# A state-space scan in front of routed experts: the operands B and C turned by TensorE, the two halves of the product matrix interleaved

## The chip, the cores and the metric

One core of one Trainium2 chip runs the kernel. The metric is device time in microseconds (us) of one execution. The kernel is one launch; nothing is computed on the host.

## What is computed

The first half is a state-space scan (Mamba-2 style) over 4 batches x 8 heads x 768 tokens with head size D = 32 and state size N = 16; the second half sends each of the 3072 tokens to one of 8 experts, by a hash of its id.

```python
log_a = np.log(np.clip(a, 1e-06, 1.0))
for c in range(nc):                                   # chunks of tokens
    cum = np.cumsum(la, axis=-1)
    L = np.exp(cum[..., :, None] - cum[..., None, :]) * causal
    M = einsum('bhin,bhjn->bhij', Cc, Bc) * L
    y = M @ xc + einsum('bhin,bhnd->bhid', Cc, state) * exp(cum)
    state = exp(sum(la)) * state + sum_j B_j x_j exp(cum[-1] - cum_j)
x = y.transpose(0, 2, 1, 3).reshape(3072, 256)
expert_idx = token_ids * 2654435761 % 8
out[mask_e] = np.maximum(x[mask_e] @ w1[e], 0) @ w2[e]   # w1 256x1024, w2 1024x256
```

## The kernel before, in words

**Scan.** The kernel works in units of T = 64 tokens. Two units make a product step k (128 tokens, `NPR` = 6 of them), two product steps make a load step ck (CT = 256 tokens, `CK` = 3). A unit's decay factors exp(-cum) and exp(cum) are multiplied into the rows of B and C (`scale_rows`, L206, line of the operation L208), so that the decay mask falls out of the product.

The decays: `a` is loaded as 96 rows (batch, head, ck) of 256 tokens (L104). DVE clips it, ACT takes the log, DVE makes running sums (L188) and centres them (L191), 32 small TensorE products bring them to the layout of B and C (L196) and ACT makes `fac` (L201, L202). Two ACT table loads stand in this chain.

B and C (`raw`, L110 to L113) lie with tokens on the partitions. They are scaled, then turned by DVE's 32x32 stream transposes into `bt` and `ct` (`turn_rows`, L218); ACT makes from `ct` two copies `ce` in which the even or the odd head of a pair is zeroed (`mask_c`, L224). After this turn, the 32 partitions of strip b hold batch b, and 4 column groups g hold pairs of heads. B is also needed with tokens as rows: eight DMAs per load step, issued on ACT's queue, copy the scaled rows to `ben` (`shuffle_b`, L229).

A product step then has these parts on TensorE, all fp32, each matmul call being two records in the trace:
- `gram` (L503): 32 calls, 32 rows x 64 columns of the array, 128 moving columns: C times B. The order is g, u (unit), b, so that eight tiles of the array (four strips b, two column halves u) are used in turn.
- `masked` (L508): one DVE instruction copies the causal part of four PSUM banks to `m_sb`.
- `dstates` (L521): 32 calls, new state contributions; ACT evicts `d_sb` (L527); `states` on DVE (L537, L540) chains the states z.
- `intra` (L556): 64 calls of 64x64, 32 moving columns; m times x.
- `inter` (L568): 64 calls of 32x64, 32 moving columns, one a head: masked C times z.
- `y_evict` on ACT (L575), `y_store` on SP's DMA queue (L578) to `y_dram`.

The order is written out by hand (L580 to L669): in step k, `states(k)`, `masked(k+1)`, `intra(k)`, `inter(k)`, `y_evict(k)`, a piece of the routing, after k = 0 and k = 2 the turn of the next load step, `gram(k+2)`, `dstates(k+1)`. Each engine executes its instructions in this order. POOL scales the rows of load steps 1 and 2. x is loaded as four DMAs per 128 tokens on SP (L118).

**Routing.** Between the steps, DVE, POOL and TensorE count the tokens of each expert, sort the experts by size, give each token a slot, and build the tables `idx_in` and `idx_out` (L259 to L420): ids, counts (before k = 0), prefix (k = 0), places and ranks (k = 1), slots, lanes and tiles (k = 2), the table product (L396) and the index arithmetic (k = 3). Seven gathers of early tiles (`EK`, tokens of the first 2048 rows of y) are issued on POOL after step 4 in program order (L664); after the scan TensorE turns them (`turn_pair`, L467).

**Experts.** From L745 on, the experts' two layers are done by a Strassen scheme with seven products per 2x2 block (`up` L745, `down` L790; sums on DVE and POOL, L701 to L726), weights loaded on SP (L435, L439). The weight loads after the first few wait for the gather of the late tiles, by a small DMA `held` (L866). Its end is a scatter of the output rows on POOL (L826). This part is in the change only at its start.

Each TensorE result lands in one of eight PSUM banks of 128 x 512 fp32: `gram` in 0 to 3, y in 4 to 7, `dstates` in halves of 6 and 7.

Of the kernel before, what the change touches and what calls it, by code (L numbers as in the profile page):

```python
# [9 lines left out]
F32 = mybir.dt.float32  # L10
# [15 lines left out]
def kernel(  # L26
# [61 lines left out]
    BM, BY, BD, SP = 0, 4, 6, 256  # L88
# [15 lines left out]
    tok = apre.tile([NCH, P, 2], I32)  # L106
    raw, xs = {}, {}

    def load_rows(ck, i, eng):
        t = raw[ck, i] = aload.tile([P, H, RR * NS], F32, name=f"raw{i}")  # L110
        for b in range(NB):
            src = (B, C)[i][b, :, ck * CT:(ck + 1) * CT, :].rearrange("h (p r) n -> p h (r n)", r=RR)
            eng.dma_start(out=t[32 * b:32 * b + 32], in_=src)  # L113

    def load_x(k):
        t = xs[k] = xload.tile([P, NB, H, D], F32, name="x_t")
        for b in range(NB):
            sp_e.dma_start(out=t[:, b], in_=x[b, :, k * P:(k + 1) * P, :].rearrange("h t d -> t h d"))  # L118

    load_rows(0, 0, sp_e)  # L120
    load_rows(0, 1, act)
    act.dma_start(out=tok, in_=tok_h.bitcast(I32).rearrange("(c p two) -> c p two", c=NCH, two=2))
    load_x(0)
    load_x(1)

    fill16 = const.tile([P, 512], BF16)
    dve.memset(fill16, 0.0)
    rst = apre.tile([P, CT // T, T], F32)
# [4 lines left out]
    m_sb = [awork.tile([P, NB, G * 2 * T], F32, name=f"m{i}", bufs=1) for i in range(2)]  # L133
    ident = const.tile([P, P], F32)
    make_identity(nc, ident)
    dve.memset(m_sb[0], 0.0)
    cmask = apre.tile([P, 2 * G, T], F32)
    pool_e.memset(cmask, 1.0)
    for u in range(2):
        pool_e.affine_select(out=cmask[u * T:(u + 1) * T], in_=cmask[u * T:(u + 1) * T], pattern=[[0, 2 * G], [1, T]],  # L140
                             compare_op=OP.is_ge, fill=0.0, base=0, channel_multiplier=-1)
    par = apre.tile([P, 2], F32)
    dve.tensor_reduce(out=par, in_=ident.rearrange("q (b e n) -> q e b n", b=NB, e=2), axis=AX.XY, op=OP.add)
    rep = apre.tile([NA, NB * 2, NS], F32)
    reph = apre.tile([NA, NB * 2], F32)
    idn = ident[0:NA, 0:NA].rearrange("q (b g e c) -> q b g e c", b=NB, g=G, e=2)
    for b in range(NB):
        dve.tensor_reduce(out=reph[:, 2 * b:2 * b + 2], in_=idn[:, b].rearrange("q g e c -> q e g c"), axis=AX.XY,
                          op=OP.add)
# [887 lines left out]
```

## Time and profile before

| what | us |
|---|---|
| median of 3 runs | 297.62 (297.23 to 301.02) |
| profiled execution, its time | 296.71 |
| its span, first to last instruction | 295.0 |
| around the span | 1.71 |
| PE busy | 232.9 (79%) |
| DVE / POOL / ACT busy | 194.0 / 166.7 / 72.2 |

An engine is busy while one of its instructions executes; idle time before an instruction is put down to what released it. PEld is TensorE's weight load, which runs beside PE. PEclk, or the granted clock, is a share of 2.4 GHz; it has two levels, 1.0 and 0.5 (1.2 GHz), and values between are means.

### The profile page before, as it was taken

To read this page: it belongs to the slowest core of one execution; us is meant where nothing else is said; L and a number is where in the kernel's file an instruction comes from. 1 tells how busy PE (TensorE), PEld (TensorE's weight loads), DVE (VectorE), ACT (ScalarE), POOL (GpSimd) and SP (SyncE) were. 2 spreads that over 40 slices of the span, in tenths; PEclk is the share of its full clock that TensorE was granted. 3 is DMA by queue.
4 is the path that set the end of the run, shared out by engine and by line. 5 is a ranking of instruction groups with operands and counts; after the bars stand their busy time and mean duration, and the time that the engine had idled before them with its cause. 6 is when DMAs were issued, how large, how long until landed. Compare 5 with 4: busy or idle time off the path is not lost.

```text
span 295.0 us, 7905 instructions
## 1 busy us (share of the span) xinstructions
PE 232.9 (79%) x3314; PEld 217.4 (74%) x3315; DVE 194.0 (66%) x316; ACT 72.2 (24%) x152; POOL 166.7 (57%) x181
## 2 busy tenths in 40 slices
PE   6347579270695588969799989999999998699980
PEld 2136469270594477959799989999999898699870
DVE  4758829369156110427987997896878979876710
ACT  2330221010311012644122123223242340342110
POOL 5304204138604500649995997999969999064123
PEclk9655555555559555999999999999999999999998
DMA  8999983734005322498418164292141421220001
GB/s 166 153 175 143 174 175 79 145 110 144 2 6 174 97 76 74 124 292 317 158 31 289 39 195 164 54 298 76 37 155 42 115 105 37 84 78 36 20 35 56
DMA packets 53371, 34.87 MB, mean 118 GB/s; under 512 B 27068, under 2 KB 47668, under 8 KB 53334
## 3 DMA queue, kind: packets, MB, share of 16 engines
q1 hardware_dynamic: 46242, 25.69, 33.5%
q0 software_dynamic: 2400, 6.43, 6.7%
q10 hardware_dynamic: 4692, 2.22, 4.3%
q8 instruction: 27, 0.44, 0.6%
q14 instruction: 10, 0.08, 0.1%
HBM read 26.47 MB, written 6.42 MB: 111 GB/s over the span
## 4 chain that ended last, share of the span: by engine, by line
PE 40%; DVE 21%; DMA 17%; issue 9%; ACT 4%; POOL 3%; SPq 2%; ACTq 2%; POOLq 0%; DVEq 0%
PE ps L745 13%; PE ps L790 13%; DMA out_dram<-o_sb,idx_out 9%; DVE t L710 4%; PE ps L568 4%; DMA w<-in_moe_w_dram 4%; DVE m L508 3%; PE ps L556 3%; PE ps L503 3%; ACT ce L224 2%; DMA raw<-in_C_dram 2%; DMA x_t<-in_x_dram 2%; ACTq L229 2%; PE ps L521 2%; SPq L118 1%
## 5 line engine op out<-in xcount | busy, mean ns | idle before, releaser
L447 POOL DMA_INDIRECT xg<-y_tokens,idx_in x25 | 29.2, 1169 | 36.7 <-DMA y_tokens<-y_sb 18.0
L701 POOL TENSOR_TENSOR s<-w 128x512 f32<-128x512 f32 x30 | 38.7, 1292 | 13.3 <-DMA w<-in_moe_w_dram 12.9
L826 POOL DMA_INDIRECT out_dram<-o_sb,idx_out x25 | 29.1, 1164 | 25.4 <-ACT o_sb L822 17.7
L745 PE MATMUL ps<-t,s 128*128 128x202 f32 (+7 forms) x192 | 37.2, 327 | 1.6 <-DVE u L760 1.6
L790 PE MATMUL ps<-t,s 128*128 128x202 f32 (+7 forms) x192 | 35.3, 326 | 0.2 <-DVE t L722 0.2
L745 PEld LDWEIGHTS ps<-t,s 128*128 128x128 f32 x192 | 31.6, 189 | 2.2 <-issue 1.9
L790 PEld LDWEIGHTS ps<-t,s 128*128 128x128 f32 x192 | 31.8, 189 | 0.4 <-issue 0.4
L556 PE MATMUL ps<-x_t,m 64*64 64x32 f32 x768 | 22.4, 282 | 9.4 <-ACT d_sb L527 5.7
L556 PEld LDWEIGHTS ps<-x_t,m 64*64 64x64 f32 x768 | 20.7, 209 | 11.4 <-ACT d_sb L527 6.2
L503 PE MATMUL ps<-ce,bt 32*64 32x128 f32 x384 | 13.2, 416 | 20.0 <-ACT ce L224 18.5
L503 PEld LDWEIGHTS ps<-ce,bt 32*64 32x64 f32 x384 | 10.8, 209 | 21.0 <-ACT ce L224 19.2
L745 PE MATMUL ps<-xT,w 128*128 128x202 f32 (+7 forms) x128 | 24.5, 327 | 1.6 <-DMA w<-in_moe_w_dram 1.6
L568 PE MATMUL ps<-z,ce 32*64 32x32 f32 x704 | 20.5, 290 | 3.0 <-issue 3.0
L537 DVE TENSOR_TENSOR zd<-d_sb,z 128x256 f32<-128x256 f32 x10 | 4.2, 425 | 27.5 <-ACT d_sb L527 27.4
L745 PEld LDWEIGHTS ps<-xT,w 128*128 128x128 f32 x128 | 21.0, 190 | 1.8 <-issue 1.8
L568 PEld LDWEIGHTS ps<-z,ce 32*64 32x64 f32 x704 | 18.7, 217 | 4.4 <-issue 4.0
L710 DVE TENSOR_TENSOR t<-xT 128x202 f32<-128x202 f32 (+7 forms) x16 | 19.2, 1198 | 4.0 <-ACT xT L461 4.0
L701 POOL TENSOR_TENSOR s<-w,s 128x512 f32<-128x512 f32 x15 | 20.4, 1363 | 0.2
L701 POOL TENSOR_TENSOR s<-s,w 128x512 f32<-128x512 f32 x15 | 19.9, 1325 | 0.7
L575 ACT ACTIVATE y_sb<-ps 128x1024 f32<-128x1024 f32 x6 | 6.1, 1024 | 50.4 <-PE ps L568 50.4
L208 POOL TENSOR_TENSOR rows<-raw,fac 128x1024 f32<-128x1024 f32 x5 | 10.7, 2149 | 13.3 <-DMA raw<-in_C_dram 8.8
L773 ACT ACTIVATE hx<-hx 128x404 f32<-128x404 f32 (+7 forms) x16 | 8.2, 524 | 40.6 <-DVE hx L772 36.8
(178 smaller groups left out, 460.2 us busy)
## 6 DMA issues: line engine op xcount, KB each, us to landing
w<-in_moe_w_dram SPq DMA_DIRECT2D x16, 512.0 KB, 8.0
w<-in_moe_w_dram SPq DMA_DIRECT2D x8, 1024.0 KB
x_t<-in_x_dram SPq DMA_DIRECT2D x24, 128.0 KB, 4.6
y_tokens<-y_sb SPq DMA_DIRECT2D x6, 512.0 KB, 2.9
raw<-in_B_dram SPq DMA_DIRECT2D x12, 128.0 KB, 3.3
ben<-rows ACTq DMA_DIRECT2D x24, 64.0 KB, 2.4
raw<-in_C_dram SPq DMA_DIRECT2D x8, 128.0 KB, 4.0
raw<-in_C_dram ACTq DMA_DIRECT2D x4, 128.0 KB
```

Of the source, the lines that this page charges most:

```text
L208: eng.tensor_tensor(out=t.rearrange("q r (h n) -> q r h n", h=H), in0=raw[ck, i].rearrange("q h (r n) -> q r h n", r=RR), in1=fac[:, i].re ...
L447: pool_e.indirect_dma_start(out=xg[k], out_offset=None, in_=y_dram[0:n, :], in_offset=bass.IndirectOffsetOnAxis(ap=idx_in[:, k:k + 1], axi ...
L503: pe.matmul(out=ps[u * T:(u + 1) * T, BM + b, g * P:(g + 1) * P].rearrange("q (e i) -> q e i", e=2), lhsT=bts[ck][r, g, c], rhs=ces[ck][r, ...
L508: dve.copy_predicated(out=m_sb[k % 2], mask=cmask.bitcast(I32).rearrange("q j i -> q (j i)").unsqueeze(1).to_broadcast([P, NB, 2 * G * T]) ...
L556: pe.matmul(out=o, lhsT=m_sb[k % 2][u * T:(u + 1) * T, b, h * T:(h + 1) * T], rhs=xs[k][u * T:(u + 1) * T, b, h], start=first, stop=True, ...
L568: pe.matmul(out=o, lhsT=ces[ck][r, h // 2, h % 2, kk * P + u * T:kk * P + (u + 1) * T], rhs=zs[2 * k + u][r, h * D:(h + 1) * D], start=fir ...
L701: eng.tensor_tensor(out=s[:, i], in0=a_, in1=b_, op=o)
L710: dve.tensor_tensor(out=t[:, i], in0=a_, in1=b_, op=OP.subtract)
L745: pe.matmul(out=ps[:, bank, i * n:(i + 1) * n], lhsT=lhs[:, (q0 + i) * P:(q0 + i + 1) * P], rhs=rhs, start=(first and i == 0), stop=True, ...
L773: act.activation(hq(2), hq(2), AF.Relu)
L790: pe.matmul(out=ps[:, bank, 0:n], lhsT=lhs(q), rhs=rhs(q), start=(first and q == 0), stop=True, skip_group_check=True)
L826: st = pool_e.indirect_dma_start(out=out[:], out_offset=bass.IndirectOffsetOnAxis(ap=idx, axis=0), in_=o_sb, in_offset=None, bounds_check= ...
```

## The change

B and C are turned by full 128x128 transposes on TensorE (`squares`), eight for each of B and C in a load step, and evicted from PSUM by ACT or DVE (`take_b`, `take_c`), the masking of the even or odd head being done in the eviction. Batches and pairs of heads change places: the strip of 32 partitions now is the pair g, and the column group is the batch. B with tokens as rows comes from eight more transposes of `bt` (`steps_b`) instead of DMAs. The decays are computed in the layout of B and C (running sums over 8 tokens on each partition, then two products that add what lies before); so `a` is loaded by four DMAs with rows of 8 tokens (32 bytes) instead of one. The even/odd masking for the states is in `gm`, so `inter` needs one call for two heads: 32 calls of 64 moving columns in place of 64 of 32. `gram` and `masked` are cut in two halves, g = 2, 3 and g = 0, 1 (`two_halves`; `between(k)` is `intra(k, (0, 1))`), and in even steps each half of `gram(k+1)` stands between halves of `intra(k)`. POOL makes most constants and zeroes `m_sb`. x is one DMA per 128 tokens. The token ids are loaded first and counted before the decays; the routing is cut in nine pieces (6 is the table product, 7 makes `idx_in`), the seven early gathers stand after step 3, and the last two groups of early turns among the first expert products. `w2` moves to another pool.

```diff
-    a_t = apre.tile([NA, CT], F32)
-    act.dma_start(out=a_t, in_=a.rearrange("b h (c t) -> (b h c) t", c=CK))
+    act.dma_start(out=tok, ...)
+    a_t = apre.tile([P, H, CK, RR], F32)
+    for b in range(NB):
+        (sp_e, act)[b % 2].dma_start(out=a_t[32 * b:32 * b + 32],
+                                     in_=a[b].rearrange("h (c p r) -> p h c r", c=CK, r=RR))
...
+        sp_e.dma_start(out=t.rearrange("q b h d -> q (b h) d"),
+                       in_=x[:, :, k * P:(k + 1) * P, :].rearrange("b h t d -> t (b h) d"))
     load_rows(0, 0, sp_e)
-    load_rows(0, 1, act)
+    load_rows(0, 1, sp_e)
     load_x(0)
+    load_rows(1, 0, sp_e)
+    load_rows(1, 1, sp_e)
     load_x(1)
+    load_x(2)
...
+    def decays_b():
+        dve.tensor_tensor_scan(out=f2(cum), data0=rst..., data1=f2(a_t), initial=0.0, op0=OP.mult, op1=OP.add)
+        dve.tensor_copy(out=cnt..., in_=ps[:, 6, 0:2 * E * NCH])
+        pe.matmul(out=ps[:, 3, 0:NA], lhsT=ident, rhs=f2(cum), start=True, stop=False, skip_group_check=True)
+        pe.matmul(out=ps[:, 3, 0:NA]..., lhsT=wsel[:, 0]...,
+                  rhs=f3(cum)[:, :, RR - 1:RR].to_broadcast([P, HC, RR]), start=False, stop=True, ...)
+        for i in range(2):
+            act.activation(f2(fac[:, i]), ps[:, 3, 0:NA], AF.Exp, scale=(-1.0, 1.0)[i])
...
-        dve.transpose(out=t.rearrange("q g (p r) -> q g r p", r=RR),
-                      in_=rows[ck, i].rearrange("q r (g f) -> q g r f", g=G))
-            act.activation(ces[ck][:, :, e], cts[ck], AF.Copy, scale=par[:, e:e + 1])
-            eng.dma_start(out=t[:, j], in_=rows[ck, 0][16 * j:16 * j + 16])
+    def squares(ck, i, r0=0, r1=RR, bank=None):
+        for r in range(r0, r1):
+            pe.transpose(out=ps[:, bank + r // 4, (r % 4) * P:(r % 4 + 1) * P], in_=rows[ck, i][:, r], identity=ident)
...
+    def gram(k, gs=(0, 1, 2, 3)):
         for b in range(NB):
+            for u in range(2):
+                for g in gs:
+                    r = slice(32 * g, 32 * g + 32)
+                    pe.matmul(out=ps[u * T:(u + 1) * T, GB + g, b * P:(b + 1) * P]..., lhsT=bts[ck][r, b, c],
+                              rhs=ces[ck][r, :, b, c], start=True, stop=True, skip_group_check=True)
...
+    def intra(k, gs=(2, 3, 0, 1)):
+        for g in gs:
+            for b in range(NB):
+                for e in range(2):
+                    for u in range(2):
+                        r = slice(u * T, (u + 1) * T)
+                        pe.matmul(out=ps[r, YB + g, (2 * b + e) * D:(2 * b + e + 1) * D],
+                                  lhsT=m_sb[k % 2][r, g, b, e * T:(e + 1) * T], rhs=xs[k][r, b, 2 * g + e], ...)
+    def inter(k):
+        for u in range(2):
+            for b in range(NB):
+                for g in range(G):
+                    pe.matmul(out=ps[u * T:(u + 1) * T, YB + g, 2 * b * D:2 * (b + 1) * D],
+                              lhsT=cts[ck][r, b, kk * P + u * T:kk * P + (u + 1) * T],
+                              rhs=zs[2 * k + u][r, b]..., ...)
...
+    def two_halves(k, inner=None):
+        gram(k, (2, 3))
+        masked(k, 2, 4)
+        if inner:
+            inner()
+        gram(k, (0, 1))
+        masked(k, 0, 2)
...
     for k in range(NPR):
+        states(k)
+        if k % 2 == 0:
+            intra(k, (2, 3))
+            two_halves(k + 1, lambda: between(k))
+            inter(k)
+            y_evict(k)
+            y_store(k)
+            if k + 2 < NPR:
+                squares(ck + 1, 1)
+                take_c(ck + 1, 0, act)
+                squares(ck + 1, 0)
+                take_b(ck + 1)
+            dstates(k + 1)
...
+        else:
+            intra(k)
+            if nxt:
+                steps_b(ck + 1, GB, 0, 4)
+            inter(k)
+            y_evict(k)
+            y_store(k)
+            if k == 3:
+                piece(6)
+                piece(7)
+            if nxt:
+                two_halves(k + 1)
...
+                dstates(k + 1)
...
+        if k == 3:
             for q in EK:
                 gather(q, early=True)
...
+    load_w1(0, 1)
+    early(0)
+    early(1)
     a_ctx.close()
...
     for m, (what, i) in enumerate(seq):
+        if m == 3:
+            early(2)
+        if m == 6:
+            early(3)
```

## Rows read from the trace of the kernel before

**Rows 1.** Three stretches: us, busy (instructions) per engine, granted clock, DMA share, GB/s.

```profile
0.00:20.70 20.70, 9.15 (x86) 4.40 (x87) 13.40 (x37) 6.07 (x11) 6.94 (x40) 0.72 1.01 162
20.70:115.40 94.70, 61.77 (x2232) 55.82 (x2232) 48.26 (x87) 14.53 (x19) 30.70 (x38) 0.54 0.48 106
115.40:295.00 179.60, 161.93 (x996) 157.19 (x996) 132.32 (x192) 51.59 (x124) 129.05 (x103) 0.98 0.37 119
```

**Rows 2.** The same view, four stretches of the scan (PE, PEld, DVE, ACT, POOL).

```profile
33.40:38.20 4.80, 0.01 (x2) 0.01 (x3) 2.51 (x2) 3.20 (x3) 0.00 (x0) 0.50 0.95 192
51.80:58.00 6.20, 0.86 (x14) 0.58 (x8) 1.63 (x7) 0.59 (x1) 0.70 (x1) 0.50 0.76 120
64.70:76.10 11.40, 0.00 (x0) 0.00 (x0) 8.23 (x16) 3.21 (x3) 9.22 (x17) 0.50 0.32 93
92.30:102.40 10.10, 4.25 (x73) 3.25 (x73) 4.33 (x7) 0.00 (x0) 7.25 (x7) 0.61 0.33 99
```

**Rows 3.** The chain that ended last, pieces in the scan: start, us, what.

```profile
35.95 2.19 ACT ce L224 x2
53.93 3.47 DMA ben<-rows
92.27 2.84 issue
```

**Rows 4.** Timeline of the start: start, us, engine, line, operation.

```profile
4.86 0.23 DVE L184 TENSOR_SCALAR a_t<-a_t 96x256 f32<-96x256 f32 x1
5.79 1.28 ACT L132 ACT_TABLE_LOAD   x1 [5.79 <-DMA raw<-in_C_dram]
10.55 1.23 DVE L208 TENSOR_TENSOR rows<-raw,fac 128x1024 f32<-128x1024 f32 x1 [1.42 <-ACT fac L201]
20.70 2.02 PE L503 MATMUL ps<-ce,bt 32*64 32x128 f32 x64 [2.19 <-ACT ce L224]
```

**Rows 5.** DMA: the queue of SP's loads (packets, MB, share); a stretch of input loads.

```profile
q1 hardware_dynamic: 46242, 25.69, 33.5%
...
21.00:31.00 10.00, 8.52 (x315) 7.50 (x306) 7.98 (x8) 0.72 (x2) 4.26 (x3) 0.50 0.98 154
```

**Rows 6.** Groups by line and shape, 0 to 120 us.

```profile
L568 PE MATMUL ps<-z,ce 32*64 32x32 f32 x704 | 20.5, 290 | 3.0 <-issue 3.0
L503 PE MATMUL ps<-ce,bt 32*64 32x128 f32 x384 | 13.2, 416 | 20.0 <-ACT ce L224 18.5 <-DVE m L508 1.5
```

**Rows 7.** Timeline of PE and PEld: transposes, and products at both levels of the clock.

```profile
38.19 2.01 PE L503 MATMUL ps<-ce,bt 32*64 32x128 f32 x64 [4.87 <-ACT ce L224]
80.01 3.43 PE L556 MATMUL ps<-x_t,m 64*64 64x32 f32 x120 [0.38 <-ACT d_sb L527]
86.42 1.67 PE L503 MATMUL ps<-ce,bt 32*64 32x128 f32 x59
90.55 1.72 PE L556 MATMUL ps<-x_t,m 64*64 64x32 f32 x104 [0.30 <-ACT tabacc L398]
115.40 1.57 PEld L467 LDWEIGHTS ps<-ident,xg 128*128 128x128 f32 x8 [1.33 <-ACT y_sb L575]
```

**Rows 8.** Stretches around the rise of the clock (clock third from the end).

```profile
38.20:51.80 13.60, 13.28 (x512) 12.00 (x512) 9.37 (x20) 1.62 (x2) 3.52 (x3) 0.50 0.59 121
...
84.00:86.00 2.00, 2.00 (x100) 2.00 (x96) 1.05 (x2) 0.00 (x0) 0.00 (x0) 0.50 0.00 0
90.00:92.00 2.00, 1.70 (x110) 1.59 (x107) 1.30 (x9) 0.21 (x1) 0.00 (x0) 1.00 0.98 251
```

**Rows 9.** An expert product in the chain; the weight loads of its line (the page's groups).

```profile
205.36 1.30 PE ps L790 x8
...
L790 PEld LDWEIGHTS ps<-t,s 128*128 128x128 f32 x192 | 31.8, 189 | 0.4 <-issue 0.4
```

**Rows 10.** Timeline after the scan: first late gather, then the first product held by weights.

```profile
119.41 1.00 POOL L447 DMA_INDIRECT xg<-y_tokens,idx_in  x1 [18.03 <-DMA y_tokens<-y_sb]
...
130.87 0.89 PE L745 MATMUL ps<-xT,w 128*128 128x192 f32 x4 [1.62 <-DMA w<-in_moe_w_dram]
```

More of the change, by code (lines that the diff above doesn't have):

```diff
@@ L226, in shuffle_b @@
[L226 to L229 removed]
+    UC = CT // T
+    usel = apre.tile([P, UC + 1, NB], F32)
+    pool_e.memset(usel, 1.0)
+    sel(usel[:, 0:UC], [[-RR, UC], [-32, NB]], -RR // 2, 1)
+    sel(usel[:, 0:UC], [[RR, UC], [32, NB]], RR + RR // 2 - 1, -1)
+    sel(usel[:, 0:UC], [[0, UC], [32, NB]], 31, -1)
+    sel(usel[:, UC], [[-32, NB]], 0, 1)
@@ new lines, with first @@
+    begun = set()
+    def first(g, u):
+        f = (g, u) not in begun
+        begun.add((g, u))
+        return f
+    def intra(k, gs=(2, 3, 0, 1)):
+        for g in gs:
+            for b in range(NB):
+                for e in range(2):
+                    for u in range(2):
+                        r = slice(u * T, (u + 1) * T)
+                        pe.matmul(out=ps[r, YB + g, (2 * b + e) * D:(2 * b + e + 1) * D],
+                                  lhsT=m_sb[k % 2][r, g, b, e * T:(e + 1) * T], rhs=xs[k][r, b, 2 * g + e],
+                                  start=first(g, u), stop=True, skip_group_check=True)
@@ L543 @@
-    begun = set()
-    def y_out(b, u, h):
-        o = (u + b) % 2
-        first = (b, o) not in begun
-        begun.add((b, o))
-        return ps[o * T:(o + 1) * T, BY + b, h * D:(h + 1) * D], first
-    def intra(k):
-        for h in range(H):
-            for b in range(NB):
-                for u in range(2):
-                    o, first = y_out(b, u, h)
-                    pe.matmul(out=o, lhsT=m_sb[k % 2][u * T:(u + 1) * T, b, h * T:(h + 1) * T],
-                              rhs=xs[k][u * T:(u + 1) * T, b, h], start=first, stop=True, skip_group_check=True)
@@ new lines @@
+    scale_rows(dve, 0, 0, 0, 4)
+    squares(0, 0, 0, 4)
+    scale_rows(dve, 0, 0, 4, 8)
+    filler(1)
+    squares(0, 0, 4, 8)
+    scale_rows(dve, 0, 1, 0, 4)
+    squares(0, 1, 0, 4, YB)
+    scale_rows(dve, 0, 1, 4, 8)
+    squares(0, 1, 4, 8, YB)
+    take_b(0)
+    dve.tensor_reduce(out=par, in_=ident.rearrange("q (b e n) -> q e b n", b=NB, e=2), axis=AX.XY, op=OP.add)
+    take_c(0, 1, dve, 1, YB)
+    take_c(0, 0, act, 0, YB)
+    take_c(0, 0, dve, 1, YB)
+    take_c(0, 1, act, 0, YB)
@@ new lines, with between @@
+    steps_b(0, 6, 0, 4)
+    piece(1)
+    two_halves(0)
+    for e in range(2):
+        act.activation(gm[:, :, :, e], g_sb, AF.Copy, scale=par[:, e:e + 1])
+    take_c(0, 2, act, None, YB)
+    dstates(0)
+    consts_late()
+    iota_n = iota([P, P], [[1, P]])
+    iota_c1 = iota([P, NCH], [[1, NCH]], base=1)
+    iota_p = iota([P, 1], [[0, 1]], mult=1)
+    load_rows(2, 0, sp_e)
+    load_rows(2, 1, sp_e)
+    load_x(3)
+    scale_rows(pool_e, 1, 0)
+    scale_rows(pool_e, 1, 1)
+    def between(k):
+        intra(k, (0, 1))
```

493 lines of the change are left out of this document (239 added, 254 removed).

## The prediction

> **What bounds the kernel now.** I read the busy time by stretch first. The span falls into a start of 20.7 us, the six scan steps up to 115.4 us, and 179.6 us of expert work behind them [rows 1]. In the last stretch PE is busy for 161.9 of 179.6 us at a granted clock of 0.98: that part is TensorE's, and the change hardly touches it. In the scan PE is busy 61.8 of 94.7 us at a mean clock of 0.54, so 32.9 us are idle. No other engine is near its limit there: DVE 48.3, POOL 30.7, ACT 14.5 us.
>
> Next I asked where PE stands still. Three stretches hold 21.5 of the 32.9 us: 4.8 us from 33.4, 5.3 us (6.2 less 0.86) from 51.8, and all 11.4 us from 64.7 [rows 2]. The chain of waits names what ended them: DVE's stream transposes and then ACT's masked copies before step 2's gram, and the copies of B to `ben`, on whose issue ACT is held up [rows 3]. In the third stretch DVE does routing, then the same transposes. A fourth, from 92.3 to 102.4, is of another kind: PE is busy 4.25 of 10.1 us, and the chain says "issue", so that PE waits for no engine that the profile shows; POOL issues its seven gathers just then [rows 2, 3]. The remaining 5.5 us are short hand-overs. So the scan is bound by latency: a turn of B and C stands serially before every second product.
>
> **The start.** Before, DVE takes `a` at 4.86, `fac` lets the first row scaling begin at 10.55, and the first gram begins at 20.70 [rows 4]: 10.15 us for scaling, DVE turning, DMAs on ACT's queue and masking. After, `a` comes in 3072 pieces of 32 bytes. No row shows such a piece. Bounds: the stretch from 21 to 31, at a DMA share of 0.98, moves 154 GB/s in pieces mostly of 128 and 512 bytes; at 128 bytes each, that is 13 ns of one engine's time. The mean over SP's queue is 0.335 x 16 x 295 us / 46242 = 34 ns [rows 5]. So 3072 / 16 pieces take 2.5 to 6.6 us. I take 4.2, between them, since these pieces are the smallest but pay their fixed cost in full. With two issues on each queue before it and the landing, `a` is there at about 7.7, some 3 us later than now (1 to 5 as bounds). Both table loads remain (1.28 us each); the first is done by then, as ACT's queue issues three DMAs rather than six before it. From the end of the first table load before (5.79 + 1.28 = 7.07) to the scaling at 10.55, log, second table load, running sum, products and exponential take 3.5 us [rows 4]; after `a`, the same chain ends at 11.2. The routing prefix, six small DVE operations, stands in the gap in which DVE waits for it, and I let DVE begin at 11.3; if the prefix is not hidden, some 1 us more. Four half scalings at about 0.63 (half of 1.23, [rows 4]) end at 13.9; the transposes follow each half, at 1.57 / 8 = 0.196 us each on the lower clock [rows 7]; the last C squares end at 14.8, and two halves of C on DVE and on ACT, 0.6 to 0.7 us each, end at 16.4. First gram at 16.4 instead of 20.7: **-4.3 us**.
>
> **PE's work in the scan.** Added: 24 transposes for a load step; those of steps 1 and 2 fall in this stretch, 48 x 0.196 = **+9.4**. Bounds: half that on the upper clock, and nothing below it.
> Removed: half of inter's 704 records. They take 20.5 / 704 = 29 ns each [rows 6]; the new ones have 64 moving columns. For a column take [rows 9]: 1.30 us for 8 products of 192 columns at the upper level, 0.85 ns a column and record, so 1.7 ns at the lower. 64 columns are 108 ns, in four tiles in turn 27 ns, below the 29 of the row. So 352 x 29 = 10.2, **-10.3**.
> Gram keeps its 384 records, at 13.2 / 384 = 34 ns [rows 6], but its halves use two strips and two column halves, four tiles in turn where eight were. A record of 128 columns holds its tile 216 ns at the lower level; over four tiles that is 54 ns, 20.7 us in all: **+7.5**. Bounds: zero, if the eight tiles were not what set 34 ns (on the upper clock 59 records take 1.67 us, 28 ns, so something else sets a floor there, [rows 7]), and 15 if the column halves give nothing. I take the four tiles, as the old row (31 ns, [rows 7]) lies close to its own bound of 216 / 8 = 27.
> Intra keeps 768 records of 32 columns. It now alternates between two tiles instead of four: 54 / 2 = 27 ns as bound, and the old row has 3.43 / 120 = 29 [rows 7]. **0**; it could lose up to 29 ns a record (22 us) if a tile's weight load didn't run beside its own product, against which [rows 9] speak: 8 products end every 1.30 us while their loads, 189 ns each or 1.51 us in all, run beside them on the same strips. The Trainium skill says otherwise, in "TensorE: Matmul & The Clock Gate", Part 3: Packing small matmuls: a weight load overlaps products in flight only where the row group differs. By these rows the trace doesn't agree, and the sum stands; by the rule it would be the slower case below.
> Dstates is the same. Sum: 61.8 + 9.4 - 10.3 + 7.5 = 68.4 us.
>
> **Idle time that stays.** The 21.5 us go. DVE's transposes leave; ACT gets five evictions per load step for them, at 1.1 us (half of the 2.19 for two masked copies, [rows 3]), beside some 23 us of PE work. They stand after inter in an even step, while a whole intra follows before the next gram needs them: hidden by that intra; without it each load step would pay these 5.5 us. `ben` comes by PE and ACT, also behind that intra. POOL's scaling of load step 1 must wait for its B and C, now queued before x1: `a`, two load steps of B and C at 1.05 MB and x0 at 0.52 MB are 2.7 MB, 17.7 us at 154 GB/s [rows 5], so there by some 21 us; with POOL's operation taken as twice DVE's 1.23 [rows 4], scaled by 26, and needed at about 29. The cover is thin, and 3 us are lost if it's gone. Routing pieces stand behind masks on DVE, not between B and gram. The early gathers move one step up but beside the same PE work: I keep the 5.9 us of the stretch from 92.3, and the 5.5 us of hand-overs, and add 1.2 us: six more waits of PE for DVE by the halves, at about 0.2. What is queued behind them is the other half of intra, which in even steps fills them. Idle: 12.6 us.
>
> **After the scan.** The next products wait for the store of y, the late gathers at 119.41, the small held DMA and weights that land at 130.87 [rows 10]. None of these is moved against the last `y_evict`; two turn groups less before the first product save 1.6 us that are waited for at 130.87 anyway. So 0, and the 179.6 us stay. `w2` in another pool waits for buffers of the scan, long free: 0. SP's queue: x as one DMA issues the same rows; each x now stands behind the y store in program order, with some 10 us in hand.
>
> **The sum on the present clock**: start 16.4, scan 68.4 + 12.6 = 81.0, experts 179.6, together 277.0; with 1.7 around the span 278.7.
>
> **The clock.** The stretch from 38.2 to 51.8 is dense and stays at 0.50; the one from 76 with PE hardly idle is at 0.50 until 86 and at 1.00 from 88 to 92, and falls again in the gap [rows 2, 8]. On the upper level, intra takes 1.72 / 104 = 16.5 ns a record in place of 29 [rows 7]: 768 x 12 = 9.3 us; gram 384 x (54 - 28) = 10.0; inter 4.2 by intra's ratio; transposes, if halved, 4.7: 28 us if all of the scan were on it. PE would be busy 68 of 81 us (84%, now 65%), in unbroken runs longer than any now, and so I expect more of the upper level, but as the dense 13.6 us without it show, not all of it. I take a third: -9.3.
> **Forecast: 278.7 - 9.3 = 269.4 us**, against 296.71 of the profiled execution, which is 0.9 below the median shown; I leave that difference in the range. A measurement of this kernel tells about 2% (5.9 us) from no change.
>
> **Rivals.**
> *The clock stays low* (as from 38.2 to 51.8): 278.7. For it: 13.6 us with PE busy for 13.28 didn't raise it. Against it: the next stretch, hardly denser, did [rows 8].
> *The clock rises for the whole scan*: 278.7 - 28 = 250.7. Against it: the gathers' gap must not break it.
> *Instruction supply*: PE, now dense, runs dry as from 92 to 102 in four places rather than one: 278.7 + 3 x 5.9 = 296.4, no change. For it: the chain's "issue" beside the gathers. Against it: from 21 to 31, with DMA as full, there was no such gap [rows 5].
> *Slower: two strips don't overlap.* In the new gram, successive calls in a strip would pay their own weight load and product in turn: 216 + 189 ns over two strips, 202 ns a record instead of 54, +57 us: 326. The gain is gone at 125 ns a record (27.3 / 384 = 71 more), 2% are lost at 141. For it: four tiles instead of eight, which no row shows; against it [rows 9].
> That the change doesn't do what it says (the turn stays on the path, since TensorE must do it) is the part of the 9.4 us above.
>
> **How the numbers follow.** Forecast 0.50; low clock 0.23; high clock 0.15; instruction supply 0.06; strips 0.06. Faster by over 2%: the first three, 0.88; within 2%: 0.06; slower: 0.06. The range: below, the high clock's 250.7 is reached only if nothing else takes over, and I go to 256; above, the low clock plus the upper bounds of `a` and POOL's cover, 278.7 + 2.4 + 3 = 284. 256 to 284 leaves out both last rivals and a part of the high clock, about 0.2.
>
> **What would show it.** First gram near 16.4; no PE gap above 4 us in the scan except beside the gathers; squares near 0.2 us (0.1 on the upper clock); a gram half of 32 records at 1.7 us on the lower clock, 0.9 on the upper; the last `y_evict` ending at 86 to 89; from there to the end 179 to 181 us. It is wrong if intra takes over 5 us a step, if PE waits for rows of POOL or for x at each step, or if the experts' stretch grows.

## The result, and the profile after

| what | before | after |
|---|---|---|
| median of 4 runs each, same chip, us | 299.32 (297.23 to 301.28) | 289.67 (288.37 to 290.21) |
| ratio after / before | | 0.9672, 95% interval 0.9581 to 0.9764 |
| profiled execution, its time / span | 296.71 / 295.0 | 288.37 / 286.7 |
| last `y_evict` ends, from the span's start | 115.36 | 103.34 |

The change made the kernel faster by 3.3%. The forecast was 269.4 us with a range of 256 to 284: the direction is right, the time is 20.3 us above the forecast and outside the range. Times of the same kernel differed by a few per cent between chips and executions, so below kernels are set against their neighbours on one chip, the places inside the traces count more than single times, and a ratio to before leaves out executions over 1.5% above a kernel's fastest, which medians keep.

The three stretches of after, cut at the first gram and at the end of the last `y_evict`, answer to [rows 1]; columns as there (us, busy of PE, PEld, DVE, ACT, POOL, granted clock, DMA share, GB/s):

```profile
0.00:14.40 14.40, 10.43 (x54) 6.02 (x55) 9.98 (x29) 6.72 (x12) 11.56 (x53) 1.00 1.12 142
14.40:103.34 88.94, 74.63 (x1934) 67.59 (x1935) 37.04 (x77) 21.28 (x28) 32.54 (x41) 0.71 0.57 110
103.34:286.70 183.36, 163.19 (x992) 158.51 (x990) 136.17 (x192) 50.95 (x125) 128.65 (x103) 0.97 0.36 117
```

The profiled execution missed its forecast by 288.4 - 269.4 = 19.0 us. By stretch: the start -2.0 (14.40 for 16.4), the scan +17.2 (88.94 for 81.0 - 9.3 = 71.7), the experts +3.8 (183.4 for 179.6). So the question is the scan; there PE is busy 74.6 us where 68.4 - 9.3 = 59.1 were forecast, and idle 14.3 where 12.6 were.

PE's groups in the scan, by line and shape (records, busy us, mean ns, idle us before them and what ended it), answer to [rows 6] and [rows 3]:

```profile
L342 PE MATMUL ps<-x_t,m 64*64 64x32 f32 x768 | 33.4, 248 | 8.9 <-issue 8.8
L289 PE MATMUL ps<-ce,bt 32*64 32x128 f32 x384 | 18.8, 337 | 3.8 <-issue 3.3 <-DVE pick L440 0.5
L354 PE MATMUL ps<-z,ct 32*64 32x64 f32 x352 | 9.9, 299 | 0.0
L243 PE MATMUL ps<-ident,rows 128*128 128x128 f32 x32 | 6.4, 384 | 0.0
L308 PE MATMUL ps<-x_t,ben 64*32 64x64 f32 x352 | 5.6, 232 | 2.1 <-ACT y_sb L363 1.2 <-issue 0.6 <-ACT ct L263 0.3
L273 PE MATMUL ps<-ident,bt 128*128 128x128 f32 x16 | 2.9, 343 | 0.0
```

Two things are to be seen. Intra (L342) is busy 33.4 us, the largest group by far; the forecast had 768 x 29 ns less a third of 9.3, 19.2 us. And of 14.3 idle us, 8.8 + 3.3 + 0.6 = 12.7 are "issue": PE waits for no engine. The waits for ACT's masked copies and for `ben` of [rows 2, 3] are gone.

PE's timeline at both levels of the clock, against [rows 7] (start, us, engine, line, operation, records): a gram half and intra at the lower level, intra and a whole gram at the upper, intra at the lower again. Below it are the stretches of the three intra runs, with the granted clock third from the end:

```profile
21.86 1.98 PE L289 MATMUL ps<-ce,bt 32*64 32x128 f32 x32
23.77 3.62 PE L342 MATMUL ps<-x_t,m 64*64 64x32 f32 x64
...
33.70 3.68 PE L342 MATMUL ps<-x_t,m 64*64 64x32 f32 x118
...
73.53 1.65 PE L289 MATMUL ps<-ce,bt 32*64 32x128 f32 x64
...
93.60 7.04 PE L342 MATMUL ps<-x_t,m 64*64 64x32 f32 x128
```
```profile
23.70:27.30 3.60, 3.60 (x68) 3.49 (x64) 1.29 (x1) 0.00 (x0) 0.00 (x0) 0.50 0.90 126
32.90:38.00 5.10, 4.60 (x187) 4.39 (x188) 4.31 (x12) 3.68 (x5) 3.84 (x7) 1.00 1.19 192
93.60:100.50 6.90, 6.90 (x132) 6.90 (x128) 0.85 (x2) 0.38 (x1) 0.00 (x0) 0.50 0.51 149
```

An intra record takes 7.04 / 128 = 55 ns at the lower level and 3.68 / 118 = 31 at the upper; [rows 7] had 29 and 16.5. It nearly doubled at both.

The chain that ended last, its pieces from 33.77 to 50.8 (start, us, what), shows the gaps:

```profile
33.77 3.61 PE ps L342 x118
37.38 0.50 issue
37.88 0.53 PE ps L342 x10
38.41 1.02 PE ps L273 x8
39.43 0.90 PE ps L354 x53
...
40.43 0.95 PE ps L289 x41
41.37 1.88 issue
43.25 0.86 PE ps L289 x18
44.12 0.79 PE ps L308 x53
44.90 1.91 PE ps L342 x45
46.82 2.73 issue
49.54 1.27 PE ps L342 x19
```

Between the gaps at 37.38 and at 41.37 the full program has 10 records of intra, 8 transposes, 64 of inter and 46 of gram, 128 products and as many weight loads. Between 41.37 and 46.82 it has 18 of gram, 64 of dstates and 45 of intra, 127. So these gaps stand 256 records of PE apart. The gaps that the chain shows at 18.52, 66.62, 75.94 and 81.00 fit the same grid: 383 products lie between 18.52 and 37.38 and between 46.82 and 66.62, then 256 up to 75.94 and 127 up to 81.00. But not every end of 256 records has a gap: those inside the 383 and the 256 have none.

### The profile page after: what moved, and what is told of

The parts are those of the page before. It is cut to its first block, busy times and chain, and to the rows that moved or that the text cites. A ratio compares the mean times of both kernels' runs of the same rounds, so it can differ in the third digit from the quotient of the medians.

```text
span 286.7 us, 7200 instructions
## 1 busy us (share of the span) xinstructions
PE 248.3 (87%) x2978; PEld 232.1 (81%) x2978; DVE 183.2 (64%) x296; ACT 79.0 (28%) x162; POOL 172.7 (60%) x197
## 4 chain that ended last, share of the span: by engine, by line
PE 56%; issue 16%; DVE 13%; DMA 5%; POOL 5%; ACT 2%; SPq 1%; POOLq 1%; ACTq 0%; DVEq 0%
PE ps L841 14%; PE ps L886 13%; PE ps L342 11%; PE ps L289 6%; DVE t L806 4%; DMA w<-in_moe_w_dram 4%; POOL out_dram L922 3%; PE ps L243 3%; PE ps L354 3%; PE ps L308 2%; DVE hx L868 1%; PE ps L273 1%; DMA a_t<-in_a_dram 1%; PE ps L913 1%; DVE t L818 1%
## 5 line engine op out<-in xcount | busy, mean ns | idle before, releaser
L797 POOL TENSOR_TENSOR s<-w 128x512 f32<-128x512 f32 x30 | 38.7, 1292 | 14.3 <-DMA w<-in_moe_w_dram 13.9
L342 PE MATMUL ps<-x_t,m 64*64 64x32 f32 x768 | 33.4, 248 | 8.9 <-issue 8.8
L342 PEld LDWEIGHTS ps<-x_t,m 64*64 64x64 f32 x768 | 31.4, 168 | 11.2 <-issue 10.7
L295 DVE COPY_PREDICATED m<-cmask,ps 128x1024 f32<-128x1024 int32 x12 | 15.3, 1296 | 29.7 <-PE ps L289 29.6
L841 PE MATMUL ps<-xT,w 128*128 128x202 f32 (+7 forms) x128 | 25.9, 336 | 1.0 <-DMA w<-in_moe_w_dram 1.0
L841 PEld LDWEIGHTS ps<-xT,w 128*128 128x128 f32 x128 | 21.9, 197 | 1.5 <-ACT xT L601 1.2
L289 PE MATMUL ps<-ce,bt 32*64 32x128 f32 x384 | 18.8, 337 | 3.8 <-issue 3.3
L797 POOL TENSOR_TENSOR s<-w,s 128x512 f32<-128x512 f32 x15 | 20.2, 1345 | 0.2
L289 PEld LDWEIGHTS ps<-ce,bt 32*64 32x64 f32 x384 | 13.8, 167 | 6.4 <-issue 5.3
L886 PE MATMUL ps<-t,w 128*128 128x202 f32 (+7 forms) x64 | 13.0, 349 | 4.1 <-DVE du L903 4.0
L820 DVE SCALAR_TENSOR_TENSOR t<-hx 128x808 f32<-128x808 f32 (+7 forms) x8 | 16.3, 2042 | 0.0
L886 PEld LDWEIGHTS ps<-t,w 128*128 128x128 f32 x64 | 11.1, 199 | 5.2 <-DVE du L903 5.2
```

Of the source, the lines that this page charges most:

```text
L289: pe.matmul(out=ps[u * T:(u + 1) * T, GB + g, b * P:(b + 1) * P].rearrange("q (e i) -> q e i", e=2), lhsT=bts[ck][r, b, c], rhs=ces[ck][r, ...
L295: dve.copy_predicated(out=m_sb[k % 2][:, g0:g1].rearrange("q g b i -> q g (b i)"), mask=cmask.bitcast(I32).rearrange("q j i -> q (j i)").u ...
L342: pe.matmul(out=ps[r, YB + g, (2 * b + e) * D:(2 * b + e + 1) * D], lhsT=m_sb[k % 2][r, g, b, e * T:(e + 1) * T], rhs=xs[k][r, b, 2 * g + ...
L797: eng.tensor_tensor(out=s[:, i], in0=a_, in1=b_, op=o)
L820: dve.scalar_tensor_tensor(out=t[:, 2], in0=q(0, 1), scalar=0.0, in1=q(1, 1), op0=OP.max, op1=OP.subtract)
L841: pe.matmul(out=ps[:, bank, i * n:(i + 1) * n], lhsT=lhs[:, (q0 + i) * P:(q0 + i + 1) * P], rhs=rhs, start=(first and i == 0), stop=True, ...
```

## Experiments

**Which tiles intra uses.** Theory 1: two 64x64 tiles in turn make each tile pay its own weight load and product one after the other, where before four tiles were in turn. Before, y had a PSUM bank for each batch, and the output half was (u + b) % 2; in the change the banks go by pair, and the half is u. Its rivals: the PSUM bank (many calls in a row write to one), and the supply of instructions.

`e1_four_tiles`, in the kernel after (inter's output half likewise):
```diff
-        for g in gs:
-            for b in range(NB):
-                for e in range(2):
+        for b in range(NB):
+            for e in range(2):
+                for g in gs:
...
-                        pe.matmul(out=ps[r, YB + g, ...
+                        o = (u + g) % 2
+                        pe.matmul(out=ps[o * T:(o + 1) * T, YB + g, ...
```


> The changed kernel, but y of unit u is written to the partition half (u + g) % 2, and intra runs over batch, head, then pair g, so that four 64x64 tiles of the array are used in turn where two were. The halves of y for odd pairs g are left swapped, so those columns of the output belong to other tokens. Theory 'tiles' (a tile takes its weight load and its product one after the other, so two tiles in turn cost twice as much as four): intra falls from 55 to about 29 ns a record at the lower clock and from 31 to about 17 at the upper, 33.4 us to 18 to 22 us busy, and the time falls by 8 to 12 us against the changed kernel, to 278 to 282. Theory 'supply' alone (PE is limited by the arrival of its instructions): the time moves by less than 3 us, as the idle time put down to issue grows by what intra gives back.

`e2_banks` has only the order b, e, g, u of that edit, with the halves as in the change:

> The changed kernel with intra's loops in the order batch, head, pair, unit: the same two tiles in turn, but successive calls write to two or four PSUM banks where sixteen went to one. Theory 'tiles': no change, 55 ns a record at the lower clock, time 288 to 291. Theory 'banks' (a bank takes one product after the other): intra falls to about 29 ns, time 278 to 282.

`b1_two_tiles`, the same question put to the kernel before:
```diff
-        o = (u + b) % 2
+        o = u
```


> The kernel before, with y of unit u written to partition half u in every batch (before: (u + b) % 2). Four PSUM banks are still used in turn, but intra now alternates between two tiles. The rows of y for odd batches are other ones than the routing takes them for. Theory 'tiles': intra goes from 29 to about 55 ns a record at the lower clock, 22.4 to 33 to 40 us busy, time up by 8 to 16 us, to 305 to 313. Theory 'banks': no change, 297 to 301.

Measured: e1 284.31 us (280.23 to 285.43, 4 runs; ratio to before 0.9416, 0.9202 to 0.9631), e2 290.3 and b1 307.6 (one run each, before at a median of 301.63 on that chip). For e1 278 to 282 had been expected; the kernel after wasn't run beside it. Intra's group up to the end of the scan and one long run of it at the lower clock, in e1:

```profile
L343 PE MATMUL ps<-x_t,m 64*64 64x32 f32 x768 | 20.2, 253 | 13.9 <-issue 12.2 <-ACT d_sb L313 1.7
...
88.08 3.43 PE L343 MATMUL ps<-x_t,m 64*64 64x32 f32 x120 [0.19 <-ACT d_sb L313]
```
the group in e2:
```profile
L342 PE MATMUL ps<-x_t,m 64*64 64x32 f32 x768 | 35.4, 249 | 11.2 <-issue 9.3 <-ACT d_sb L313 1.1 <-DVE m L295 0.4
```
and the same two rows in b1:
```profile
L556 PE MATMUL ps<-x_t,m 64*64 64x32 f32 x768 | 36.6, 260 | 8.5 <-ACT d_sb L527 4.7 <-issue 3.5 <-ACT tabacc L398 0.3
...
79.72 6.61 PE L556 MATMUL ps<-x_t,m 64*64 64x32 f32 x120 [0.18 <-ACT d_sb L527]
```

Four tiles bring 33.4 us down to 20.2 and the record back to 3.43 / 120 = 29 ns, the very row of [rows 7]; rotating banks alone does nothing (35.4); taking two of the four tiles from the kernel before makes its record 55 ns. So the tiles are the cause, in both kernels, and the bank theory falls. But the last `y_evict` in e1 starts 9.1 us sooner (93.19, after: 102.32), while intra's busy time fell by 13.2. The other groups of PE took 1.4 us more, and PE's idle time in the scan grew by 2.3, to 16.6: 1.7 of it are new waits for ACT's `d_sb`, 0.6 "issue" (13.3 in all, after: 12.7). So shorter products leave the "issue" time where it was: it has a second cause.

**Whether loads of x starve PE.** `e4_x_once` loads x once and uses it in every step:
```diff
+        if k > 0:
+            xs[k] = xs[0]
+            return
```


> The changed kernel with x loaded for the first 128 tokens alone and used in all six steps: five of six loads of x are left out, and y is another one. Theory 'supply' (instructions of PE come by DMA, and wait behind other transfers): the idle time of PE put down to issue before 50 us (2.5 us from 18.5, 1.9 from 41.4, 2.7 from 46.8, 0.5 from 37.4) mostly goes, 5 to 7 us; that beside the weights and the gathers (from 66 on) stays. Time 282 to 285. Rival: the stalls belong to the instructions themselves, whatever the DMA load: the same stalls at the same instructions, time within 1.5 us of the changed kernel.

Measured: 298.22 us (one run, with 193 us behind the last `y_evict`, which nothing here explains); that evict starts at 102.15, as in after, and "issue" before intra is 9.5 us in 10 gaps. From 36 to 44 the DMA share is 0.02, and a gap of 0.46 us still stands at 43.0. Ahead of 50 us its "issue" gaps come to 4.6 us; after had 7.6, the same kernel in a second trace (r1, below) 5.3. So the traffic of x may lengthen the gaps, by no more than two traces of one kernel differ, but it doesn't make them, and the expectation that 5 to 7 us go was a miss.

**Whether PE gets its instructions in pieces.** `e5_tiny` puts 512 very short products behind inter of step 2, results unused:
```diff
+                for i in range(512):
+                    r = 32 * (i % 4)
+                    pe.matmul(out=ps[r:r + 32, 6, 256:264], lhsT=fill16[r:r + 32, 0:32], rhs=fill16[r:r + 32, 0:8], ...)
```


> The changed kernel with 512 tiny products (32x32 weights, 8 moving columns) put in after inter of step 2, where DMA is almost idle (share 0.02 from 50 to 59 us); they write to a part of PSUM that nothing reads. Each is two instructions of TensorE, so there are 1024, four pieces of 256. Theory 'supply' (instructions come in pieces of 256, each some 5 us after the one before, whatever else DMA does): PE idles by issue at every 256th instruction, four times, and the 1024 take 18 to 22 us together. Rival 'contention' (the pieces are late only behind other transfers): no idle time by issue above 0.5 us among them, and they take 10 to 14 us.

The products in PE's timeline, and the core's DMA while they run, 60 to 71 us:

```profile
59.86 1.17 PE L718 MATMUL ps<-fill 32*32 32x8 bf16 x128 [1.40 <-issue]
63.31 1.18 PE L718 MATMUL ps<-fill 32*32 32x8 bf16 x128 [2.29 <-issue]
66.77 1.19 PE L718 MATMUL ps<-fill 32*32 32x8 bf16 x128 [2.27 <-issue]
70.77 0.81 PE L718 MATMUL ps<-fill 32*32 32x8 bf16 x83 [2.82 <-issue]
```
```profile
DMA packets 3, 0.05 MB, mean 4 GB/s; under 512 B 0, under 2 KB 0, under 8 KB 0
## 3 DMA queue, kind: packets, MB, share of 16 engines
q8 instruction: 3, 0.05, 1.7%
```

Exactly 128 products and their 128 loads run in 1.2 us, then PE stands for 2.3 to 2.8 us; in these 11 us nothing moves but three packets of the instruction queue, one for each piece. In the packed trace these start at 60.90, 64.35 and 68.40 and land 0.9 to 1.1 us later; PE goes on 1.3 to 1.4 us after each landing, and each starts only 1.0 to 1.6 us after the piece before it began. So a piece of 256 comes every 3.45 to 4.0 us, with DMA idle: 27 to 31 ns for a product with its load. All 512 took 13.6 us, less than the 18 to 22 expected, as the pieces follow each other sooner than the 5 us supposed.

In the scan the pace is lower. Where after ran dry, its pieces began 5.4 (37.88 to 43.25), 6.3 (43.25 to 49.54) and 5.3 us (76.50 to 81.84) apart, 42 to 49 ns for a product with its load; the packets there start 2.3 to 3.2 us after the piece before them began, and PE goes on 1.4 to 1.6 us after they land. What delays their start isn't shown. The pace fits where the gaps are: intra with two tiles at the upper clock (31 ns) is faster than this and meets gaps, with two at the lower (55 ns) it runs without one (93.60, above).

**The stores that put four tiles right.** In e1 the halves of two pairs lie exchanged. `e6_store` exchanges them in the store of y, in six DMAs of 256-byte rows, four of them on ACT's queue; `c1_sp_store` has all six on SP's:
```diff
+        for g in range(0, G, 2):
+            sp_e.dma_start(out=d[:, :, g], in_=t[:, :, g])
+        for g in range(1, G, 2):
+            for u in range(2):
+                act.dma_start(out=d[u * T:(u + 1) * T, :, g], in_=t[(1 - u) * T:(2 - u) * T, :, g])
```


> As the run with four tiles, but the swapped halves of the odd pairs are put right by the stores of y: three DMAs a step with rows of 256 bytes in place of one with rows of 1 KB, two of them on ACT's queue. All tokens are where they belong. Theory 'tiles': the last eviction of y ends 8 to 9 us sooner than in the changed kernel (at 94 to 96 us); the last store lands 1 to 2 us later after it than before. Time 280 to 284, a ratio of about 0.94 to 0.95 to the kernel before. Rival: the smaller rows of the stores hold up weights and gathers, and the expert part grows by 5 us or more: 286 to 289.

Measured: 285.22 us (278.51 to 286.42, 4 runs; before 297.2); 280 to 284 had been expected. ACT issues the stores ahead of `d_sb`, and PE waits 5.8 us for it, in three waits. A miss of placement, mended in c1, below.

**The wait behind the scan.** In after, PE stands 2.25 us at 113.9 for the eviction of the last early turn, which DVE does only when sums that wait for w1 are done. `e7_last_turn` gives it to ACT; `e8_gathers_late` has the seven early gathers behind step 5 in the program:
```diff
-        turn_pair([...], (3, 2, 7, 6)[m], (act, dve)[m % 2])
+        turn_pair([...], (3, 2, 7, 6)[m], act if m == 3 else (act, dve)[m % 2])
```
```diff
-        if k == 3:
+        if k == 5:
             for q in EK:
                 gather(q, early=True)
```


> The changed kernel with the last early turn evicted by ACT instead of DVE, where four sums stand ahead of it that wait for weights. If that wait matters, PE's idle time of 2.25 us (from 111.65) goes and the stretch from the last eviction of y to the end shrinks from 183.4 by 1 to 2 us. If the weights that land 16.5 us after that eviction are what counts, it stays at 183 to 184.

> The changed kernel with the seven early gathers after step 5 instead of step 3. If the gathers are what makes PE wait from 81 to 89 us, the scan's last eviction of y comes 3 to 5 us sooner (98 to 100), and the first expert products wait for the gathers instead, 9 us later. If the pieces of instructions alone set it, idle time by issue in step 4 stays above 2.5 us.

Measured: 282.8 and 280.71 us, one run each on another chip, some 7 and 9 below after's median. To tell an edit from a lucky execution, the kernel after was run again, unedited, as `r1_after`, beside both edits in one kernel (`c2_late_turn`), c1, and all edits together (`c3_all`):

> The changed kernel, nothing edited, beside its three variants on one chip. Theory (PE starved of instructions, how much of it differs between executions): 280 to 290 us; gaps of PE at every 128 or 256 calls in the scan, 8 to 14 us in all, in other places than in its first trace beside the gathers; last y_evict ending at 94 to 104. Rival (the 76 to 89 us gaps of its first trace belong to the early gathers, in every execution): those gaps stand again, some 4 us, last y_evict at 102 to 104, and 289 us.

> The changed kernel with the seven early gathers behind step 5 and the last early turn evicted by ACT. Theory that gathers and PE's instruction loads get in each other's way: 6 to 9 us below the unchanged one (4 us in the scan, 2 to 4 after it). Rival (what the two single runs gained was the chip and the execution): within 2 us of the unchanged kernel; the gaps between 76 and 89 us are as small in one as in the other.

> The changed kernel with four 64x64 tiles in turn for the intra products and inter likewise in the other half for odd pairs, and the six DMAs that put y right all on SP's queue, none on ACT. Tiles theory: intra at 30 ns a record on the lower clock, last y_evict 8 to 10 us sooner than the unchanged kernel's on the same chip, and 5 to 8 us off the time, as the stores in rows of 256 bytes land 2 us later than those of 1 KB. Rival (instruction supply alone sets the scan's pace): the gaps grow by what the products lose, last y_evict at most 3 us sooner.

> Both sets of edits together: four tiles in turn with the stores on SP, gathers behind step 5, the last early turn evicted by ACT. If the two causes are separate their gains add: 10 to 16 us below the unchanged changed kernel, 272 to 280 us. If supply takes over when the products become short, the sum falls short: no more than 3 us below the better of the two.

| kernel (one chip, 4 runs each) | median us | last `y_evict` starts |
|---|---|---|
| r1_after | 292.86 (286.03 to 296.74) | 100.51 |
| c2_late_turn | 292.58 (289.69 to 297.68) | 104.38 |
| c1_sp_store | 282.99 (281.69 to 284.84) | 94.58 |
| c3_all | 287.40 (283.83 to 291.75) | 96.61 |

On this chip before took 304.92 (298.83 to 310.83, 7 runs). c2 gains nothing over r1: what e7 and e8 showed was the execution. In e7 the wait for DVE does go, but 3.1 us for the weights take its place, and from the last `y_evict` to the end it takes 186.2 us (after: 183.4), where 1 to 2 less were expected. And e8's edit moved nothing in time: POOL starts the gathers when their indices are ready, at 79.59 in e8 and 79.03 in c2 (after: 78.28), since no other work of POOL stands before them; that its last `y_evict` ends at 98.75, within the 98 to 100 expected, says nothing of the gathers. r1's median lies above the 280 to 290 expected of it. c1 has the lowest median of the table: 0.9446 of before (0.9358 to 0.9534). All its four runs lie below r1's lowest, by 1.2 to 4.3 us; the medians lie 9.9 us apart, but r1's runs spread over 10.7. Its last `y_evict` starts 5.9 us sooner than r1's, where 8 to 10 had been expected. From the first gram to that evict it is 9.3 us shorter (76.4 for 85.7); but the first gram, which no edit touches, began at 18.21 there and at 14.82 in r1. c3 adds nothing to c1; its theory had expected 272 to 280.

**What the gathers do to PE.** While the gathers are under way, r1's PE shows, in place of one long gap, a row of short ones (timeline of PE):

```profile
76.46 0.70 PE L342 MATMUL ps<-x_t,m 64*64 64x32 f32 x14
77.38 0.33 PE L342 MATMUL ps<-x_t,m 64*64 64x32 f32 x5 [0.22 <-issue]
78.14 0.32 PE L342 MATMUL ps<-x_t,m 64*64 64x32 f32 x4 [0.43 <-issue]
78.90 0.35 PE L342 MATMUL ps<-x_t,m 64*64 64x32 f32 x5 [0.43 <-issue]
...
85.45 0.87 PE L342 MATMUL ps<-x_t,m 64*64 64x32 f32 x12 [0.98 <-issue]
```

Four or five products in 0.75 us, for 9 us, in the place where after had them, as the rival in r1's expectation said. Ten traces have such rows beside the gathers: before, b1, after, r1, e1, e2, e4, c1, c2 and c3. Four haven't: e5, e6, e7 and e8, all traced together on one chip, though their gathers ran in the scan too. In e8, with gathers before and behind it, intra runs dense after a gap at a piece's end:

```profile
82.46 1.00 POOL L587 DMA_INDIRECT xg<-y_tokens,idx_in  x1 [0.30 <-issue]
82.90 1.24 PE L342 MATMUL ps<-x_t,m 64*64 64x32 f32 x37 [1.14 <-issue]
...
85.06 1.00 POOL L587 DMA_INDIRECT xg<-y_tokens,idx_in  x1 [0.30 <-issue]
```

`g1_gathers_behind_y` (from after) and `g2_four_behind_y` (from c1) move the gathers in time: they read all of y, so they wait for its last store.
```diff
-        if k == 3:
+        if k == 5:
             for q in EK:
-                gather(q, early=True)
+                gather(q)
```


> The changed kernel with the seven early gathers reading all of y, so that they wait for the store of the last step (in the edit that only moved them in the program, POOL still started them at 79 us, as nothing held it). Theory (PE's instructions trickle in while gathers are under way): the run of gaps of 0.2 to 1.0 us in step 4's intra, some 4 to 5 us in all, goes; gaps of 0.5 to 3 us at every 128 or 256 calls stay; last y_evict at 96 to 99; after it the early tiles come 9 us later, so the time is 287 to 296. Rival (the trickle is step 4's own): the gaps stay where they were and last y_evict ends at 101 to 105.

> The same with four 64x64 tiles in turn and stores on SP. Theory that gathers cause the trickle: no run of short gaps in step 4's intra, last y_evict at 88 to 92 (95.6 with the gathers in the scan); time 282 to 292, as the expert part starts later. Rival: the short gaps stay, last y_evict at 94 to 97.

Measured: 301.46 and 295.4 us, one run each (before 300.07), above the 287 to 296 and 282 to 292 expected: the early tiles come late, and PE waits 8.7 us for the first in g1, so as kernels both are worse. For the theory the scan counts. PE's timeline in step 4 of g1, and its evicts of steps 3 to 5:

```profile
78.26 1.00 PE L342 MATMUL ps<-x_t,m 64*64 64x32 f32 x27
79.86 2.10 PE L342 MATMUL ps<-x_t,m 64*64 64x32 f32 x37 [0.60 <-issue]
81.89 1.75 PE L289 MATMUL ps<-ce,bt 32*64 32x128 f32 x26
```
```profile
71.42 1.02 ACT L363 ACTIVATE y_sb<-ps 128x1024 f32<-128x1024 f32 x1 [0.56 <-PE ps L354]
85.34 1.02 ACT L363 ACTIVATE y_sb<-ps 128x1024 f32<-128x1024 f32 x1 [9.54 <-PE ps L354]
96.14 1.02 ACT L363 ACTIVATE y_sb<-ps 128x1024 f32<-128x1024 f32 x1 [8.14 <-PE ps L354]
```

One gap of 0.60 us, at a piece's end, is left. From evict 3 to evict 4 (counted from 0) it is 13.9 us, where after has 18.6 (72.90 to 91.51) and r1 19.5; g2 has 17.4, c1 23.0. So the stretch with the short gaps is 4.7 to 5.6 us longer. In the scan both came out as the theory expected, but they don't prove it: e7 and e8 have 13.9 and 12.7 us there with the gathers under way, and beside g1 and g2 no kernel with the gathers in the scan was traced. That the gaps need the gathers fits these traces; that moving the gathers took them away isn't shown.

## Why the prediction was wrong in size

**The step that failed is "Intra 0".** The prediction saw that intra goes from four tiles to two, wrote down the price if a tile's load doesn't run beside its own product (29 ns a record, 22 us), and set it to 0 because in [rows 9] loads of full-array products run beside products on the same strips. That row doesn't carry over to 64x64 tiles. Measured: 55 ns in place of 29 at the lower clock, so 26 of the 29 ns; 33.4 us in place of the 19.2 forecast, +14.2. In the net that is all but 1.3 of the 15.5 us by which PE's busy time was missed. With four tiles in turn (e1) the same products took 20.2, and from the first gram to the last `y_evict` it is 9.4 us shorter (c1 against r1: 9.3). So the step is the largest part of the 17.2 us of the scan, but not all of it. By b1, the kernel before would have shown it too. The bound of 22 us was on the page and not in the range: it had been argued away. With it the range would have reached past 289.

Successive calls alternate between the two strips of 64 partitions, with two tiles as with four. The rule of the Trainium skill that the prediction set aside ("TensorE: Matmul & The Clock Gate", Part 3: Packing small matmuls: a load overlaps products in flight only where the row group differs) speaks of the right cost, a load that isn't hidden. But as stated it doesn't tell 55 from 29 ns, since the row groups in turn are the same two in both orders. What these runs show is that the number of tiles in turn decides. That a load waits for the product before it in its own tile fits them (two tiles at 55 ns are 110 ns for each; 54 of them were the estimate for 32 columns), but no run shows it by itself.

**Idle time: the sum was right, its parts were not.** 12.6 us were forecast, 14.3 measured. But hand-overs between engines, priced at 5.5 + 1.2, cost 14.3 - 12.7 = 1.6 us, and "issue", priced at the 5.9 of the gathers' gap, cost 12.7: by the chain about 9.8 in six gaps ahead of the gathers, all on the grid of 256 records, and 3.0 beside them. That these parts sum to nearly the forecast is luck. So the rival of the instruction supply, given 0.06, was half right: PE does run dry in many places now, and the row it was read from (92.3 to 102.4, [rows 2, 3]) was of two kinds: an instruction packet lands at 93.82 and PE goes on from the long gap 1.3 us later, then the short gaps of the gathers follow. Against it stood that from 21 to 31 there was no gap; there the packets start 4.2 to 4.4 us apart (22.85, 27.23, 31.38), and 128 products of 32 ns last 4.1.

**What was right.** The turn leaves the path: the one wait for it that is left is 0.3 us, for ACT's `ct`, and the copies to `ben` are gone. The other terms, each with its part of the clock's gain taken off, came out near the forecast: transposes 6.4 + 2.9 = 9.3 (forecast 7.8), inter 9.9 (8.8), gram 18.8 (17.4). A gram half at the lower clock took 1.98 us, forecast 1.7: 62 ns a record for 54, so its four tiles do overlap, and the rival "strips don't overlap" at 202 ns is out. The clock: 0.71 in the mean, two fifths of the way from 0.5 to 1.0, forecast a third.

Two rows had been misread without much harm. The 59 gram records of 1.67 us [rows 7], taken for the upper clock, ran at a mean of 0.63; after's whole gram at the upper takes 1.65 / 64 = 26 ns, close to the 28 assumed. And the 0.196 us of a transpose came from a row of weight loads; the transposes themselves took 3.53 us for 16 at the lower clock (59.50), 0.22 each, and 1.09 for 8 at the upper (38.34), 0.14 where 0.1 was given as the sign.

**The start** was forecast at 16.4 and came at 14.40. The rows in DVE's and PE's timeline, against [rows 4]:

```profile
5.71 0.26 DVE L212 TENSOR_SCALAR a_t<-a_t 128x192 f32<-128x192 f32 x1 [0.56 <-DMA a_t<-in_a_dram]
...
9.62 2.50 DVE L235 TENSOR_TENSOR rows<-raw,fac 128x512 f32<-128x512 f32 x4
...
14.43 1.62 PE L289 MATMUL ps<-ce,bt 32*64 32x128 f32 x64 [0.52 <-DVE pick L440]
```

The 32-byte pieces of `a` land some 2 us sooner than the 7.7 that was taken: the 3072 packets of 32 bytes took 9 ns each in the trace, 1.7 us of all 16 engines, below even the 13 ns that the prediction took from larger pieces as its lower bound. The chain from there to the scaling takes 3.9 us (forecast 3.5), the rest to the first gram 4.8 (5.1). Other traces with the same start take `a` at 5.7 to 6.4 as well, but begin the first gram anywhere from 14.4 to 18.2, so the 2.0 us gained here are no more than executions differ by.

**The experts' stretch** was forecast unchanged and is 3.8 us longer. Part of it can be read: PE stands 2.25 us for DVE up to 113.9, where before its longest wait up to the first held product was 1.62 us, for weights. But the same stretch took 182.8 us in r1, 180.2 in e8, and 183.8 in b1, whose expert part is that of the kernel before. So 3.8 us is no more than executions differ by, and no cause in the change is shown. Why the four-tile kernels take longer there stays open (c1 186.9, e1 189.4): in c1 the first late gather starts 6.8 us after the last `y_evict`, behind the stores in 256-byte rows, for 4.2 in after, but in e1 it is 4.2 as well.

## What to carry to other kernels

Before products of less than the full array are laid out anew, write down for each loop which tile each successive call uses, and read the cost of a tile's own load from a row with as few tiles in turn; a row of the full array is no evidence. Removing waits from a stretch of short products runs into the pace at which instructions arrive: divide its records by 256 and multiply by 3.45 us, the least that was seen; in the scan here a piece took 5.3 to 6.3 us where PE ran dry. Do it for each dense run, not for the whole scan: over all its 1934 products the sum is 52 us, below the 74.6 that PE was busy, and the gaps were there. And a bound that rests on one argument belongs in the range.

## What the runs showed of the hardware

PE's instructions come in pieces of 256, and the next piece is not there when the last one ends quickly: 2.3 us idle with DMA empty. The Trainium skill, "Runtime: NRT & Kernel Launch", Instruction fetch mechanics, says that instructions are refilled in blocks of 256 by a DMA queue of the sequencer's own, and that the cost is mostly hidden. The size agrees with e5: three packets, 0.05 MB, one for each 128 products with their loads. The cost wasn't hidden there, nor in the scan's dry pieces, whose 128 products took 3.5 to 4.5 us and came every 5.3 to 6.3.

While gathers are under way, PE gets four or five products in 0.75 us, in ten traces of fourteen in which they ran in the scan. Late instruction packets don't explain it: r1's instruction queue moved one packet between 76 and 77 us and one between 79 and 80, e7's one between 75 and 76 and one between 78 and 79, and e7 has no such gaps although its gathers run from 74.3. So gathers alone don't bring the gaps about; that they are needed fits g1 and g2 but isn't shown, and what else is needed stays open.
